# One core: bulk loads of a spectral filter and a gated MLP moved from ScalarE's queue to SyncE's, the late ones held back to points of the matmul order

## The chip, the cores and the metric

The kernel runs on one core of a Trainium2 chip. Five engines work beside each other, each on its own instruction stream: TensorE (PE) multiplies matrices, VectorE (DVE) and ScalarE (ACT) do elementwise work, GpSimd (POOL) does small things, and SyncE (SP) issues DMAs. ScalarE can issue DMAs too; such an instruction stands in its stream like any other. The metric is the device time of one execution in microseconds.

## The reference

`x` is 2048 by 512. The result is the sum of the input, a global spectral filter of the normalised input (2D FFT, multiplication by a complex weight, inverse FFT) and a gated MLP of the normalised input:

```python
def _A_ref(x, w_r, w_i):
    X = jnp.fft.rfft2(x.astype(jnp.float32), axes=(-2, -1))
    X = X * (w_r + 1j * w_i)                              # 2048 x 257
    return jnp.fft.irfft2(X, s=(S, D), axes=(-2, -1)).astype(jnp.bfloat16)

def _B_ref(x, w_gate, w_up, w_down):                      # 512 -> 1792 -> 512
    h = _gelu(x @ w_gate) * (x @ w_up)
    return h @ w_down

xn = _layernorm(x)
return x + _A_ref(xn, A_w_r, A_w_i) + _B_ref(xn, B_w_gate, B_w_up, B_w_down)
```

## The kernel before

The rows of `x` form 16 tiles of 128, taken as four blocks of four. Each tile is normalised (`xn`), transposed by TensorE into PSUM and copied to `xnT`. For block 0 two of the four copies are VectorE's (L364) and two ScalarE's (L366); for blocks 1 to 3 all are VectorE's.

The MLP is the spine of the program: for each block b and each of 14 columns of weights fc there is a `gate` (four matmuls, a GELU on ScalarE) and an `up` (four matmuls, a product on VectorE), and from block 1 on four `down`s work off the block before. Between these stand *hooks*, numbered in order of the program: 28 in block 0, 40 in each later block. The table `plan` says which pieces of the filter are issued at which hook (`at(h, ...)`):

- `unit_D(j)` and `unit_A(j)`, hooks 4 to 43: the two forward transforms of tile j. `unit_D` needs the constants `fd`; `unit_A` needs `am` (which lies in `arena`), and ends with ScalarE's copy into one of four buffers `tt`, a store of it to the DRAM tensor `scr1`, and a load of the store before it into `tv`. Both DMAs are SP's.
- `unit_B(h)`, hooks 46 to 91: the last forward step and the multiplication by the weights. Needs all of `tv`, `be`, and `Wr`, `Wi` on VectorE.
- `unit_C(h)`, hooks 50 to 95, needs `cm`; it goes through `scr2` into `vv`. `unit_E`, `unit_F` from hook 101 on; `unit_F` needs `gm`. `down` needs `wd`, from hook 34 on.

Each engine runs its list in the order in which the Python code calls `op(engine, ...)`. `op` works out the semaphore waits from the keys an instruction reads (`r`) and writes (`w`), and puts them in front of it. A DMA is one such instruction: the engine that issues it goes on once the queue has taken it.

At the start, TensorE runs 24 matmuls on a zeroed tile `dumm` (`warm`, L327) while the first rows come in. The loads are written at the head of the function. Those of the first half of `x` and the first weight pieces are shared between SP and ScalarE; of the later ones SP has the rest of `x`, `fd` and one weight piece, ScalarE all others, 18 in all.

Of the kernel before, what the change touches and what calls it, by code (L numbers as in the profile page):

```python
# [7 lines left out]
ACT = mybir.ActivationFunctionType  # L8
# [7 lines left out]
KD = 257  # L16
FF = 1792
P = 128
NJ = 16
# [90 lines left out]
class _Prog:  # L110
# [14 lines left out]
            self.cnt[e] = 0  # L125
        self.dsem = []

    def op(self, eng, fn, r=(), w=(), dma=False):
        deps = []
        for k in r:  # L130
            if k in self.writer:
                deps.append((self.writer[k], True))
        for k in w:
            if k in self.writer:
                deps.append((self.writer[k], False))
            for ev in self.readers.get(k, ()):
                deps.append((ev, False))
        need = {}
        for (st, val), raw in deps:
            if st == eng and not dma and (eng == "pe" or not raw):  # L140
                continue
            need[st] = max(need.get(st, 0), val)
        known = self.known[eng]
        need = {s: v for s, v in need.items() if known.get(s, 0) < v}
        need = {s: v for s, v in need.items()
                if not any(s2 != s and self.clk[(s2, v2)].get(s, 0) >= v for s2, v2 in need.items())}
        for s, v in need.items():
            for a, b in self.clk[(s, v)].items():
                if known.get(a, 0) < b:
                    known[a] = b  # L150
        if dma:
            st = next((d for d in self.dsem if known.get(d, 0) >= self.cnt[d]), None)
            if st is None:
                st = "d%d" % len(self.dsem)
                self.sem[st] = self.es.enter_context(self.nc.semaphore("s_" + st))
                self.cnt[st] = 0
                self.dsem.append(st)
            self.cnt[st] += 16
            ev, inc = (st, self.cnt[st]), 16
            clk = dict(known)  # L160
        else:
            self.cnt[eng] += 1
            ev, inc = (eng, self.cnt[eng]), 1
            clk = dict(self.lastclk[eng])
            for a, b in known.items():
                if clk.get(a, 0) < b:
                    clk[a] = b
        clk[ev[0]] = ev[1]
        self.clk[ev] = clk
        if not dma:  # L170
            self.lastclk[eng] = clk
        self.q[eng].append((fn, list(need.items()), ev[0], inc))
        for k in r:
            self.readers.setdefault(k, []).append(ev)
        for k in w:
            self.writer[k] = ev
            self.readers[k] = []
        return ev
# [12 lines left out]
def bass_parallel_sum__spectral_gfnet__glu_gated_geglu__prompt_kernel(  # L191
# [12 lines left out]
    c_fd = nc.inline_tensor(FD_np, name="c_fd")  # L204
    c_am = nc.inline_tensor(AM_np, name="c_am")
    c_be = nc.inline_tensor(BE_np, name="c_be")
    c_cm = nc.inline_tensor(CM_np, name="c_cm")
    c_g = nc.inline_tensor(G_np, name="c_g")
# [5 lines left out]
    wgv = B_w_gate.rearrange("(dc p) f -> p dc f", p=P)  # L214
    wuv = B_w_up.rearrange("(dc p) f -> p dc f", p=P)
    wdv = B_w_down.rearrange("(fc p) d -> p fc d", p=P)

    with ExitStack() as es:
# [3 lines left out]
        pr = _Prog(nc, es)  # L222
        op = pr.op
# [6 lines left out]
        am = arena[:, 0:4096].rearrange("p (j r c) -> p j r c", j=NJ, r=2)  # L230
# [4 lines left out]
        wg_sb = sb("wg", [P, 4, FF], BF16)  # L235
        wu_sb = sb("wu", [P, 4, FF], BF16)
        wd_sb = sb("wd", [P, NFC, D], BF16)
        hT = [sb("hT%d" % i, [P, NFC, 512], BF16) for i in range(2)]
        ident = sb("ident", [P, P], F16)
        fd = sb("fd", [P, 768], F16)  # L240
        be = sb("be", [P, 2 * P], F16)
        cm = sb("cm", [P, 16, 2, P], F16)
        gm = sb("gm", [P, 4, 256], F16)
# [38 lines left out]
        def dma(eng, dst, src, r=(), w=()):  # L282
            return op(eng, lambda e: e.dma_start(dst, src), r=r, w=w, dma=True)  # L283

        def load_x(j0, n, b, eng):
            dma(eng, x_sb[64 * b:64 * b + 64, j0:j0 + n, :], xv[b, :, j0:j0 + n, :], w=[("x", j, b) for j in range(j0, j0 + n)])

        def load_w(t, v, nm, lo, hi, eng):
            dma(eng, t[:, :, P * lo:P * hi], v[:, :, P * lo:P * hi], w=[(nm, i) for i in range(lo, hi)])
# [8 lines left out]
        load_w(wu_sb, wuv, "wu", 0, 2, "sp")  # L298
        for b, eng in ((0, "sp"), (1, "act")):
            load_x(4, 4, b, eng)  # L300
        load_w(wg_sb, wgv, "wg", 2, 6, "sp")
        load_w(wu_sb, wuv, "wu", 2, 6, "act")
        dma("sp", fd[:], c_fd.ap(), w=["fd"])
        dma("act", am, c_am.ap().rearrange("p (j r c) -> p j r c", j=NJ, r=2), w=["am"])
        load_x(8, 4, 0, "sp")
        load_x(8, 4, 1, "sp")
        load_w(wg_sb, wgv, "wg", 6, 10, "act")
        load_w(wu_sb, wuv, "wu", 6, 10, "act")
        load_x(12, 4, 0, "sp")
        load_x(12, 4, 1, "sp")  # L310
        load_w(wg_sb, wgv, "wg", 10, 14, "act")
        load_w(wu_sb, wuv, "wu", 10, 14, "act")
        dma("act", wd_sb[:], wdv, w=["wd"])
        dma("act", be[:], c_be.ap(), w=["be"])
        for t, src, nm in ((Wr, A_w_r, "Wr"), (Wi, A_w_i, "Wi")):
            v = src.rearrange("(m hh h) k -> hh m h k", hh=2, h=16)
            for hh in range(2):
                dma("act", t[64 * hh:64 * hh + 64, :, 0:KD], v[hh], w=[(nm, hh)])
        dma("act", cm[:], c_cm.ap().rearrange("p (j r c) -> p j r c", j=16, r=2), w=["cm"])
        dma("act", gm[:], c_g.ap().rearrange("p (a c) -> p a c", a=4), w=["gm"])  # L320


        def warm(n):
# [136 lines left out]
        def unit_C(h):  # L460
            bk = 5
            y = yy[h % 4]

            def fn(e):
                ins = None
                for ri in range(2):
                    for hh in range(2):
                        ins = e.matmul(bank(bk + hh)[:, 0:257], cm[64 * hh:64 * hh + 64, h, ri, :], y[64 * hh:64 * hh + 64, ri, 0:KD],  # L468
                                       start=(ri == 0), stop=(ri == 1), skip_group_check=True)
                return ins  # L470

            op("pe", fn, r=["cm", ("yy", h % 4, 0), ("yy", h % 4, 1)], w=[("ps", bk), ("ps", bk + 1)])
            v4 = vp[h % 4]
            op("act", lambda e: e.activation(v4[:], pair(bk), ACT.Copy), r=[("ps", bk), ("ps", bk + 1)], w=[("vp", h % 4)])  # L474
            dma("sp", scr2.rearrange("(h b y) (x c) -> h (y x) b c", b=2, y=4, c=KD)[h], v4[:], r=[("vp", h % 4)], w=[("scr2", h)])
            if h > 0:
                load_vv(h - 1)
            if h == 15:
                load_vv(h)
# [100 lines left out]
        def down(b, jj):  # L580
            j = 4 * b + jj
            bk = 7

            def part(f0, f1):
                def fn(e):
                    ins = None
                    for fc in range(f0, f1):
                        ins = e.matmul(bank(bk), hT[b % 2][:, fc, jj * P:(jj + 1) * P], wd_sb[:, fc, :], start=(fc == 0), stop=(fc == NFC - 1))  # L588
                    return ins
                op("pe", fn, r=["wd"] + [("hT", b % 2, fc) for fc in range(f0, f1)], w=[("ps", bk)])  # L590

            part(0, 5)
            hook()
            part(5, 10)
            hook()
            part(10, 14)

            def add(dst, key):
                op("dve", lambda e: e.tensor_tensor(dst, bank(bk), x_sb[:, j, :], ALU.add), r=[("ps", bk), ("acc", j), ("x", j, 0), ("x", j, 1)], w=[key])  # L599
            if j in fin_done:  # L600
                store(j, lambda t, key: add(t[:], key))
            else:
                add(x_sb[:, j, :], ("acc", j))
                acc_done[j] = True
            hook()
# [5 lines left out]
        def at(h, *calls):  # L611
            plan.setdefault(int(h), []).extend(calls)
# [5 lines left out]
        def hook(fl=True):  # L618
# [3 lines left out]
            if fl:  # L622
                flush()

        for m in range(1, 4):
            a = 10 * (m - 1)
            for i in range(4):
                at(a + i, (ln_stat, 4 * m + i))
            at(a + 3, (ln_aggr, 4 * m, 4))
            for i in range(4):  # L630
                at(a + 6 + i // 2, (ln_norm, 4 * m + i))
            at(a + 8, (trans, m, (0, 1), (0, 1, 2, 3), 7))
            at(a + 9, (trans, m, (2, 3), (0, 1, 2, 3), 7))
            at(a + 10, (butter, m, 0))
            at(a + 11, (butter, m, 1))
# [88 lines left out]
```

## Time and profile before

| | |
|---|---|
| median of three executions | 251.59 us (249.69 to 252.6) |
| the profiled execution | 252.13 us, its span 250.3 us |
| granted TensorE clock, mean over the span | 0.916 |
| TensorE matmul busy | 198.6 us, 79% |
| VectorE busy | 113.3 us, 45% |
| ScalarE busy | 90.6 us, 36% |
| HBM read / written | 16.57 MB / 6.31 MB |
| SP's queue (q1) / ScalarE's queue (q10) | 13.12 MB / 9.77 MB |

The profile comes from one execution. Busy shares do not count the issuing of DMAs: an engine that is held up while it issues a load shows as idle, and its issue stands in the timeline as SPq or ACTq. The rows with two numbers in front give start and duration in microseconds; a bracket at the end gives the idle time ahead of the instruction and what ended it. The list of waits gives the total, how often, and the longest. The rows of windows give the busy time of each engine, the granted clock of TensorE, the busy share of the DMA engines and what they moved in GB/s. A chain of waits is followed back from the last instruction.

### The profile page before, as it was taken

The numbers are of one execution on the slowest core, as the hardware profiler recorded it, in microseconds if no ns is written. First come the engines' busy times: TensorE is split into PE (matmuls) and PEld (weight loads), VectorE is DVE, ScalarE is ACT, GpSimd is POOL, SyncE is SP. The second block draws the span as 40 slices with busy tenths as digits, with TensorE's granted clock in tenths as the row PEclk, the third lists the DMA queues.
The fourth block names the chain that finished last, engine by engine and source line by source line (L and its number), as shares of the span: only waits on it lengthen the run. The fifth ranks groups of instructions, "written<-read, shape, count | busy, mean of one in ns | idle before, by whom it ended". The sixth has DMA issues, their size and how long they took to land.

```text
span 250.3 us, 3084 instructions
## 1 busy us (share of the span) xinstructions
PE 198.6 (79%) x1131; PEld 89.9 (36%) x1145; DVE 113.3 (45%) x262; ACT 90.6 (36%) x157; POOL 9.3 (4%) x26
## 2 busy tenths in 40 slices
PE   8600000799999999849999999998799999999973
PEld 2300000245444444313333333343355555555421
DVE  3600000487878733206666666463046455365421
ACT  0000001654546446304445535433155446454100
POOL 0200000010101000000000000000000000000000
PEclk9965555699999999979999999999799999999999
DMA  6999999901333333300233313323001111100001
GB/s 175 294 315 291 347 155 151 240 31 43 94 78 85 84 87 84 84 21 21 53 76 84 83 47 84 81 68 84 1 12 46 31 42 43 43 21 25 21 21 42
DMA packets 23695, 23.09 MB, mean 92 GB/s; under 512 B 1920, under 2 KB 22400, under 8 KB 23168
## 3 DMA queue, kind: packets, MB, share of 16 engines
q1 hardware_dynamic: 13728, 13.12, 21.1%
q10 hardware_dynamic: 9952, 9.77, 17.0%
q8 instruction: 9, 0.15, 0.3%
q14 instruction: 6, 0.05, 0.1%
HBM read 16.57 MB, written 6.31 MB: 91 GB/s over the span
## 4 chain that ended last, share of the span: by engine, by line
PE 71%; ACTq 17%; DMA 5%; DVE 3%; ACT 1%; issue 1%
PE ps L575 19%; PE ps L588 19%; PE ps L562 18%; ACTq L283 17%; PE ps L442 2%; PE ps L468 2%; PE ps L501 2%; DMA tv<-scr 1%; PE ps L418 1%; PE ps L354 1%; DMA arena<-scr 1%; DMA scr<-tt 1%; DVE osb L599 1%; DMA scr<-vp 1%; DVE hT L578 1%
## 5 line engine op out<-in xcount | busy, mean ns | idle before, releaser
L562 PE MATMUL ps<-xnT,wg 128*128 128x512 f16 x224 | 58.8, 386 | 35.1 <-ACT xnT L366 35.1
L578 DVE TENSOR_TENSOR hT<-ps,gl 128x512 bf16<-128x512 f32 x56 | 38.6, 690 | 45.9 <-PE ps L575 41.7
L575 PE MATMUL ps<-xnT,wu 128*128 128x512 f16 x224 | 59.0, 387 | 0.0
L588 PE MATMUL ps<-wd,hT 128*128 128x512 bf16 x210 | 52.2, 388 | 3.1 <-DVE osb L599 1.9
L565 ACT ACTIVATE gl<-ps 128x512 bf16<-128x512 f32 x56 | 33.4, 597 | 42.9 <-PE ps L562 42.2
L562 PEld LDWEIGHTS ps<-xnT,wg 128*128 128x128 bf16 x224 | 20.7, 99 | 58.5 <-issue 39.9
L588 PEld LDWEIGHTS ps<-wd,hT 128*128 128x128 bf16 x224 | 20.8, 99 | 26.9 <-issue 4.1
L575 PEld LDWEIGHTS ps<-xnT,wu 128*128 128x128 bf16 x224 | 20.7, 99 | 23.0 <-issue 5.0
L376 DVE TENSOR_TENSOR arena<-xnT 128x1024 f16<-128x1024 f16 x4 | 2.8, 693 | 33.5 <-ACT xnT L366 33.4
L366 ACT ACT_TABLE_LOAD x1 | 1.3, 1283 | 42.9 <-issue 42.9
L599 DVE TENSOR_TENSOR x_sb<-ps,x_sb 128x512 bf16<-128x512 f32 x11 | 7.6, 691 | 19.9 <-PE ps L588 19.9
L448 ACT ACTIVATE xc<-ps 128x514 f16<-128x514 f32 x16 | 9.6, 600 | 15.0 <-PE ps L442 15.0
L508 ACT ACTIVATE zt<-ps 128x512 bf16<-128x512 f32 x16 | 9.5, 595 | 10.4 <-PE ps L501 10.4
L428 ACT ACTIVATE tt<-ps 128x514 f16<-128x514 f32 x16 | 9.6, 598 | 10.1 <-PE ps L422 10.1
L535 ACT ACTIVATE eo<-ps 128x512 bf16<-128x512 f32 x16 | 9.5, 595 | 9.2 <-PE ps L530 9.2
L333 DVE BATCH_NORM_STATS2 st<-x_sb 128x6 f32<-128x512 bf16 x16 | 10.6, 684 | 3.8 <-DMA x_sb<-in_A_x_dram 3.8
L474 ACT ACTIVATE vp<-ps 128x514 bf16<-128x514 f32 x16 | 9.6, 598 | 7.3 <-PE ps L468 7.3
L401 ACT ACTIVATE xs<-ps 128x512 f16<-128x512 f32 x16 | 9.5, 596 | 4.3 <-PE ps L397 4.3
L442 PE MATMUL ps<-tv,be 128*64 128x257 f16 x64 | 6.8, 294 | 4.4 <-DMA tv<-scr 4.4
L509 POOL COPY zt<-xn 1x128 bf16<-1x128 bf16 x16 | 4.5, 283 | 146.9 <-ACT zt L508 146.9
L327 PE MATMUL ps<-dumm 128*128 128x512 f16 x24 | 8.2, 524 | 1.2 <-DVE dumm L291 1.2
L540 DVE TENSOR_TENSOR ys<-eo 128x256 bf16<-128x256 bf16 x16 | 4.6, 289 | 9.3 <-ACT eo L535 9.3
(59 smaller groups left out, 156.9 us busy)
## 6 DMA issues: line engine op xcount, KB each, us to landing
scr<-tt SPq DMA_DIRECT2D x16, 128.5 KB
tv<-scr SPq DMA_DIRECT2D x16, 128.5 KB
scr<-vp SPq DMA_DIRECT2D x16, 128.5 KB
arena<-scr SPq DMA_DIRECT2D x16, 128.5 KB
out_dram<-osb SPq DMA_DIRECT2D x32, 64.0 KB
wd<-in_B_w_down_dram ACTq DMA_DIRECT2D x1, 1792.0 KB, 16.7
wu<-in_B_w_up_dram ACTq DMA_DIRECT2D x3, 512.0 KB, 17.3
x_sb<-in_A_x_dram SPq DMA_DIRECT2D x5, 256.0 KB, 15.0
```

The source lines that it names most:

```text
L283: return op(eng, lambda e: e.dma_start(dst, src), r=r, w=w, dma=True)
L333: op("dve", lambda e: e.bn_stats(st[:, j, :], x_sb[:, j, :]), r=[("x", j, 0), ("x", j, 1)], w=[("st", j)])
L428: op("act", lambda e: e.activation(t4[:], pair(bk), ACT.Copy, scale=SC_A), r=[("ps", bk), ("ps", bk + 1)], w=[("tt", j % 4)])
L442: ins = e.matmul(bank(bk + ri)[64 * hh:64 * hh + 64, 0:257], be[:, 64 * ri:64 * ri + 64], tv[:, 16 * hh + h, :], start=True, stop=True, sk ...
L448: op("act", lambda e: e.activation(xc[s2][:, :, 0:KD], pair(bk), ACT.Copy, scale=SC_B), r=[("ps", bk), ("ps", bk + 1)], w=[("xc", s2)])
L474: op("act", lambda e: e.activation(v4[:], pair(bk), ACT.Copy), r=[("ps", bk), ("ps", bk + 1)], w=[("vp", h % 4)])
L562: ins = e.matmul(bank(bg), wg_sb[:, dc, fc * P:(fc + 1) * P], xnT[:, dc, b * 512:(b + 1) * 512], start=(dc == 0), stop=(dc == 3))
L565: op("act", lambda e: e.activation(gl[k % 2][:], bank(bg), ACT.Gelu_apprx_tanh), r=[("ps", bg)], w=[("gl", k % 2)])
L575: ins = e.matmul(bank(bu), wu_sb[:, dc, fc * P:(fc + 1) * P], xnT[:, dc, b * 512:(b + 1) * 512], start=(dc == 0), stop=(dc == 3))
L578: op("dve", lambda e: e.tensor_tensor(hT[b % 2][:, fc, :], bank(bu), gl[k % 2][:], ALU.mult), r=[("ps", bu), ("gl", k % 2)], w=[("hT", b % ...
L588: ins = e.matmul(bank(bk), hT[b % 2][:, fc, jj * P:(jj + 1) * P], wd_sb[:, fc, :], start=(fc == 0), stop=(fc == NFC - 1))
L599: op("dve", lambda e: e.tensor_tensor(dst, bank(bk), x_sb[:, j, :], ALU.add), r=[("ps", bk), ("acc", j), ("x", j, 0), ("x", j, 1)], w=[key])
```

## The change

The loads of the head, but for the first four of ScalarE, are written for SP, in the order in which they are needed. ScalarE gets a GELU on one column of `dumm` in their place. The loads of `wd` (in four pieces), `be`, `Wr`, `Wi`, `cm` (in two pieces) and `gm` are taken out of the head and entered in the plan, at hooks 10 to 52: `load_late` issues them from SP with a wait until TensorE has finished everything that stands ahead of this hook. `wd` and `cm` get keys by piece, so that their readers wait for the piece they need.

```diff
-    def op(self, eng, fn, r=(), w=(), dma=False):
-        deps = []
+    def op(self, eng, fn, r=(), w=(), dma=False, after=()):
+        deps = [(ev, True) for ev in after]
...
+        def load_late(dst, src, keys):
+
+            op("sp", lambda e: e.dma_start(dst, src), w=keys, dma=True, after=[("pe", pr.cnt["pe"])])
...
             load_x(4, 4, b, eng)
+        op("act", lambda e: e.activation(dumm[:, 0:1], mhalf[:, 0:1], ACT.Gelu_apprx_tanh), r=["mhalf"], w=["dumm"])
+        dma("sp", fd[:], c_fd.ap(), w=["fd"])
         load_w(wg_sb, wgv, "wg", 2, 6, "sp")
-        load_w(wu_sb, wuv, "wu", 2, 6, "act")
-        dma("sp", fd[:], c_fd.ap(), w=["fd"])
-        dma("act", am, c_am.ap().rearrange("p (j r c) -> p j r c", j=NJ, r=2), w=["am"])
+        load_w(wu_sb, wuv, "wu", 2, 6, "sp")
         load_x(8, 4, 0, "sp")
         load_x(8, 4, 1, "sp")
-        load_w(wg_sb, wgv, "wg", 6, 10, "act")
-        load_w(wu_sb, wuv, "wu", 6, 10, "act")
+        dma("sp", am, c_am.ap().rearrange("p (j r c) -> p j r c", j=NJ, r=2), w=["am"])
+        load_w(wg_sb, wgv, "wg", 6, 10, "sp")
+        load_w(wu_sb, wuv, "wu", 6, 10, "sp")
         load_x(12, 4, 0, "sp")
         load_x(12, 4, 1, "sp")
-        load_w(wg_sb, wgv, "wg", 10, 14, "act")
-        load_w(wu_sb, wuv, "wu", 10, 14, "act")
-        dma("act", wd_sb[:], wdv, w=["wd"])
-        dma("act", be[:], c_be.ap(), w=["be"])
-        for t, src, nm in ((Wr, A_w_r, "Wr"), (Wi, A_w_i, "Wi")):
-            v = src.rearrange("(m hh h) k -> hh m h k", hh=2, h=16)
-            for hh in range(2):
-                dma("act", t[64 * hh:64 * hh + 64, :, 0:KD], v[hh], w=[(nm, hh)])
-        dma("act", cm[:], c_cm.ap().rearrange("p (j r c) -> p j r c", j=16, r=2), w=["cm"])
-        dma("act", gm[:], c_g.ap().rearrange("p (a c) -> p a c", a=4), w=["gm"])
+        load_w(wg_sb, wgv, "wg", 10, 14, "sp")
+        load_w(wu_sb, wuv, "wu", 10, 14, "sp")
...
-            op("pe", fn, r=["cm", ("yy", h % 4, 0), ("yy", h % 4, 1)], w=[("ps", bk), ("ps", bk + 1)])
+            op("pe", fn, r=[("cm", h), ("yy", h % 4, 0), ("yy", h % 4, 1)], w=[("ps", bk), ("ps", bk + 1)])
...
-                op("pe", fn, r=["wd"] + [("hT", b % 2, fc) for fc in range(f0, f1)], w=[("ps", bk)])
+                op("pe", fn, r=[("wd", fc) for fc in range(f0, f1)] + [("hT", b % 2, fc) for fc in range(f0, f1)], w=[("ps", bk)])
...
+        for i in range(4):
+            f0, f1 = (0, 4, 8, 11, 14)[i:i + 2]
+            at(10 + 2 * i, (load_late, wd_sb[:, f0:f1, :], wdv[:, f0:f1, :], [("wd", fc) for fc in range(f0, f1)]))
+        at(18, (load_late, be[:], c_be.ap(), ["be"]))
+        for i, (t, src, nm) in enumerate(((Wr, A_w_r, "Wr"), (Wi, A_w_i, "Wi"))):
+            v = src.rearrange("(m hh h) k -> hh m h k", hh=2, h=16)
+            for hh in range(2):
+                at(19 + 3 * (2 * hh + i), (load_late, t[64 * hh:64 * hh + 64, :, 0:KD], v[hh], [(nm, hh)]))
+        cmv = c_cm.ap().rearrange("p (j r c) -> p j r c", j=16, r=2)
+        for i in range(2):
+            at(31 + 3 * i, (load_late, cm[:, 8 * i:8 * i + 8], cmv[:, 8 * i:8 * i + 8], [("cm", h) for h in range(8 * i, 8 * i + 8)]))
+        at(52, (load_late, gm[:], c_g.ap().rearrange("p (a c) -> p a c", a=4), ["gm"]))
```

What moves shows best in the engines' lists. The rows give the line, the operation, what it writes and reads, its shape, and the semaphores it waits for. First ScalarE before, from the eleventh of its 18 loads up to the first GELU. `wd` is the down weight, `be`, `cm`, `gm` constants, `Wr` and `Wi` the filter's weights, `xnT` the transposed input and `gl` the GELU's output:

```order
L283 DMA wd<-in_B_w_down_dram 128x14x512
L283 DMA be<-c_be 128x256
L283 DMA Wr<-in_A_w_r_dram 64x16x257 x2
L283 DMA Wi<-in_A_w_i_dram 64x16x257 x2
L283 DMA cm<-c_cm 128x4096
L283 DMA gm<-c_g 128x1024
L366 ACT_TABLE_LOAD
L366 ACTIVATE xnT<-ps 128x2x256 [waits s_pe] x2
L565 ACT_TABLE_LOAD
L565 ACTIVATE gl<-ps 128x512 [waits s_pe] x2
```

And ScalarE after, from its start:

```order
L283 DMA x_sb<-in_A_x_dram 64x1024 x2
L283 DMA wg<-in_B_w_gate_dram 128x4x256
L283 DMA x_sb<-in_A_x_dram 64x2048
L305 ACT_TABLE_LOAD [waits s_dve]
L305 ACTIVATE dumm<-mhalf 128x1 [waits s_pool]
L363 ACTIVATE xnT<-ps 128x2x256 [waits s_pe] x2
L562 ACTIVATE gl<-ps 128x512 [waits s_pe] x2
```

Fourteen loads are gone from ahead of the copies, and one table load stands ahead of both instead of one ahead of each. On TensorE the start reads like this before, where `dumm` is the zeroed tile of the warm-up:

```order
L327 MATMUL ps<-dumm 128x512 [waits s_dve]
L327 MATMUL ps<-dumm 128x512 x23
L354 MATMUL ps<-ident,xn 128x128 [waits s_dve,s_d4]
L354 MATMUL ps<-ident,xn 128x128 x7
L354 MATMUL ps<-ident,xn 128x128 [waits s_dve]
```

And after:

```order
L324 MATMUL ps<-dumm 128x512 [waits s_act]
L324 MATMUL ps<-dumm 128x512 x23
L351 MATMUL ps<-ident,xn 128x128 [waits s_dve,s_d4]
L351 MATMUL ps<-ident,xn 128x128 x7
L351 MATMUL ps<-ident,xn 128x128 [waits s_dve]
```

The order is the same; the first matmul waits for ScalarE in place of VectorE. SP, in the stretch of the first unit_A tiles (`scr` is the DRAM scratch, `tt` and `tv` what is stored to it and loaded from it), before:

```order
L283 DMA fd<-c_fd 128x768
L283 DMA x_sb<-in_A_x_dram 64x2048 x4
L283 DMA scr<-tt 128x2x257 [waits s_act] x2
L283 DMA tv<-scr 8x8224 [waits s_d0]
L283 DMA scr<-tt 128x2x257 [waits s_act]
L283 DMA tv<-scr 8x8224 [waits s_d1]
L283 DMA scr<-tt 128x2x257 [waits s_act]
L283 DMA tv<-scr 8x8224 [waits s_d2]
```

And after, from the last loads of the head on:

```order
L283 DMA wg<-in_B_w_gate_dram 128x4x512
L283 DMA wu<-in_B_w_up_dram 128x4x512
L283 DMA scr<-tt 128x2x257 [waits s_act] x2
L283 DMA tv<-scr 8x8224 [waits s_d0]
L287 DMA wd<-in_B_w_down_dram 128x4x512 [waits s_pe]
L283 DMA scr<-tt 128x2x257 [waits s_act]
L283 DMA tv<-scr 8x8224 [waits s_d1]
L287 DMA wd<-in_B_w_down_dram 128x4x512 [waits s_pe]
L283 DMA scr<-tt 128x2x257 [waits s_act]
```

The held-back loads stand between the scr stores and tv loads, each behind a wait for TensorE (`s_pe`).

## The prediction

> **What bounds the kernel now.** I read the busy tenths of the page first, to see where TensorE stands still:
>
> ```profile
> PE   8600000799999999849999999998799999999973
> PEclk9965555699999999979999999999799999999999
> ```
>
> One slice is 6.26 us. TensorE works in slices 1 and 2, is idle from about 12 to 44 us, and from there on is nine tenths busy to the end, with two short dips. The list of waits names the hole:
>
> ```profile
> PE ps L562 <- ACT xnT L366: 35.1, 1, 35.1
> ACT L366 <- issue: 42.9, 1, 42.9
> PE ps L442 <- DMA tv<-scr: 4.4, 1, 4.4
> ```
>
> The first gate matmul (L562) waits 35.1 us for ScalarE's copy of the transposed input (L366); ScalarE itself "waits" 42.9 us for nothing but its own issue. The timeline of ScalarE says what it issues:
>
> ```profile
> 2.02 0.85 ACTq L283 DMA_DIRECT2D wg<-in_B_w_gate_dram  x1
> 2.90 0.54 ACTq L283 DMA_DIRECT2D x_sb<-in_A_x_dram  x1
> ...
> 7.16 5.39 ACTq L283 DMA_DIRECT2D wg<-in_B_w_gate_dram  x1
> 12.58 5.88 ACTq L283 DMA_DIRECT2D wu<-in_B_w_up_dram  x1
> ...
> 42.38 0.45 ACTq L283 DMA_DIRECT2D gm<-c_g  x1
> 42.86 1.28 ACT L366 ACT_TABLE_LOAD   x1 [42.86 <-issue]
> 44.15 1.08 ACT L366 ACTIVATE xnT<-ps 128x512 f16<-128x512 f16 x2
> 45.26 1.28 ACT L565 ACT_TABLE_LOAD   x1
> ```
>
> Up to 7 us a load takes ScalarE 0.5 to 1.2 us to issue; from 7.16 on each takes up to 6 us, as the queue takes new loads only as fast as old ones land. So the two copies, whose input was in PSUM at 10.3, begin at 44.15. TensorE's own rows, and VectorE's last normalisation, give what was ready when:
>
> ```profile
> 1.19 8.24 PE L327 MATMUL ps<-dumm 128*128 128x512 f16 x24 [1.19 <-DVE dumm L291]
> 8.53 0.73 DVE L345 TENSOR_SCALAR xn<-x_sb,ag,rstd 128x512 f16<-128x512 bf16 x2 [0.27 <-POOL rstd L341]
> 9.26 1.06 PE L354 MATMUL ps<-ident,xn 128*128 128x128 f16 x16
> 45.38 1.86 PE L562 MATMUL ps<-xnT,wg 128*128 128x512 f16 x4 [35.06 <-ACT xnT L366]
> ```
>
> From 45.38 to the end, 204.9 us, the kernel is bound by TensorE, and the change adds no arithmetic there. So the question is when the first gate starts, and whether the loads that it needs then keep up.
>
> **Term 1, the start of the first gate.** ScalarE keeps its first four loads, unchanged in place, so it has issued them at 2.90 + 0.54 = 3.44. Now the table load and a 128x1 GELU follow. The table load is 1.28. The shortest ACTIVATE of the trace is this:
>
> ```profile
> L489 ACT ACTIVATE row<-ps 32x64 bf16<-32x64 f32 x1 | 0.2, 212 | 2.9 <-PE ps L487 2.9
> ```
>
> I take 0.21 and end at 4.98. The GELU writes `dumm`, which the 24 warm-up matmuls read. They waited for VectorE's memset before and wait for ScalarE now: TensorE starts at about 5.1 instead of 1.19 (0.15 for the hand-over, as between the copies' end, 45.23, and the gate). This is the one cost that the change puts on the path. With 8.24 for the warm-up, TensorE gets to the transposes at 13.35, though `xn` is ready at 9.26 as before. The 16 transposes take 1.06, to 14.4. The second copy needs the last of them: half of 1.08, so 15.0, and 0.15 on top. The first gate starts at about 15.2 instead of 45.38: **30.2 us less**. Both old table loads are covered by the one new; the second cost nothing before, since its GELU waited for the gate matmuls anyway.
>
> Its bounds hang on the clock in the warm-up. The weight loads show it: they come 0.43 us apart until 7.11, then nine of them within 1.82:
>
> ```profile
> 6.71 0.15 PEld L327 LDWEIGHTS ps<-dumm 128*128 128x128 f16 x1 [0.28 <-issue]
> 7.11 1.82 PEld L327 LDWEIGHTS ps<-dumm 128*128 128x128 f16 x9 [0.25 <-issue]
> ```
>
> So TensorE was slow for 5.9 us there. The second slow stretch is shorter (columns: window, length, busy time of each engine, granted clock, DMA share, GB/s):
>
> ```profile
> 45.38:48.40 3.02, 3.02 (x9) 1.09 (x10) 1.25 (x2) 1.76 (x2) 0.00 (x0) 0.56 1.04 290
> 48.40:50.20 1.80, 1.80 (x9) 0.71 (x8) 1.60 (x4) 0.60 (x1) 0.00 (x0) 1.00 0.56 222
> ```
>
> At 0.56 of the clock, about 2.8 us were slow. With 2.8 us slow, the warm-up is 2.8/0.43 = 6.5 slow matmuls and 17.5 at 1.80/8 = 0.225, 6.7 in all: 1.5 us sooner. With 5.9 it is the 8.24. I take 8.24, the row of the same instructions, and keep 1.5 us less for the range. The Trainium skill, "TensorE: Matmul & The Clock Gate", Part 1: The HAM clock gate, says that a free-running window of about 3.4 us of activity must pass at half clock. By that the warm-up could be slow for anything from 3.4 to 6.8 us, and 8.24 could become 6.9 to 8.6. The first stretch, 5.9, agrees; the second, 2.8, is shorter than a whole window.
>
> **Term 2, the first gates at full clock.** Before, the first eight matmuls took 3.02 us where the next eight took 1.80, since TensorE had been idle for 35 us. In the changed kernel only about 0.8 us lie between the transposes and the gate, and before the clock was still up well after the transposes ended at 10.3:
>
> ```profile
> 12.00:14.00 2.00, 0.00 (x0) 0.00 (x0) 0.00 (x0) 0.00 (x0) 0.00 (x0) 0.97 1.04 409
> 14.00:16.00 2.00, 0.00 (x0) 0.00 (x0) 0.00 (x0) 0.00 (x0) 0.00 (x0) 0.50 1.06 350
> ```
>
> So these eight run at 1.80: **1.2 us less**.
>
> **Term 3, the early loads on one queue.** SP now issues all of `x`, `fd`, `am` and both weights. What TensorE needs first and could miss is `am` (1024 KB), for the first unit_A:
>
> ```profile
> arena<-c_am ACTq DMA_DIRECT2D x1, 1024.0 KB
> 53.21 0.28 PE L418 MATMUL ps<-xs,arena 64*128 64x257 f16 x2
> ```
>
> It came 7.8 us after the first gate, 6.6 without the slow clock: 21.8 in the changed kernel. Up to and with `am` both queues carry x 0..11 (1536 KB), `ident` 32, `fd` 192, the first and second weight pieces 1536 and `am` 1024: 4320 KB, 4.42 MB. The rates that the trace shows for such loads:
>
> ```profile
> 6.00:8.00 2.00, 2.00 (x9) 0.73 (x8) 1.97 (x8) 0.00 (x0) 0.99 (x2) 1.00 0.98 228
> 24.00:30.00 6.00, 0.00 (x0) 0.00 (x0) 0.00 (x0) 0.00 (x0) 0.00 (x0) 0.50 1.10 348
> 31.00:46.00 15.00, 0.62 (x2) 0.28 (x3) 0.66 (x2) 3.11 (x4) 0.00 (x0) 0.50 1.25 159
> ```
>
> From 2 us on, at 228 GB/s `am` lands at 21.4, at 348 at 14.7; the weights 10..13 (7.05 MB in all) at 32.9 or 22.3, long before their turn at hook 20. **Nothing**, between nothing and 8 us (159 GB/s puts `am` at 29.8); I take the near rows, as the 159 stretch is `Wr`, `Wi` in rows of 514 bytes. SP itself is free once its last early load is taken. If it runs three 512 KB loads ahead of the landings, as ScalarE did at 7.16 (an estimate: `wu`, `wg`, `wu` were just issued and could not have landed), that is when 5.48 MB have landed, between 17.7 and 26.0 by the two rates. The first `scr` store is due 9.05 - 1.2 = 7.9 us after the gate, at 23; up to 3 us late it holds nobody, as four `tt` buffers stand ahead of it.
>
> ```profile
> 54.43 3.89 SPq L283 DMA_DIRECT2D scr<-tt  x2
> ```
>
> **Term 4, the loads held back.** `wd`, `be`, `Wr`, `Wi`, `cm`, `gm` go to SP behind waits for TensorE's count at hooks 10 to 52. A hook takes (102.15 - 53.21)/37 = 1.32 us (last and first unit_A, hooks 43 and 6). All are long ahead of their readers: `wd` at hook 34, `Wr` at 46, `cm` at 50, `gm` at 105. The waits themselves hold nothing up: each point lies in TensorE's order ahead of the unit_A whose store stands behind it on SP. The cost can only lie in the bytes ahead of the scr stores and tv loads in the queue:
>
> ```profile
> 102.15 0.28 PE L418 MATMUL ps<-xs,arena 64*128 64x257 f16 x2
> 54.00:103.00 49.00, 47.09 (x317) 22.41 (x317) 31.46 (x66) 26.19 (x47) 2.01 (x2) 1.00 0.33 79
> 103.21 3.02 DMA scr<-tt
> 106.25 3.49 DMA tv<-scr
> ```
>
> The thick part is hooks 19 to 31, 15.9 us, with four loads of 514 KB: 13.2 us at 159 GB/s, beside 0.33 x 15.9 = 5.2 us of scr and tv traffic. The queue falls 2.5 us behind. A store then takes 3.0 (the chain's row) + 3.3 (one load ahead of it) + 2.5 = 8.8 us, and the store of unit_A(j) has to land before ScalarE writes the same of four `tt` buffers, 10 hooks or 13.2 us later. So nothing stops; and from hook 31 on only 1 MB of `cm` comes, so the lag is gone by hook 43. What may remain is a later last tv load, on which unit_B already waits 4.4 us. Bounds 0 and 3.3 (one load ahead of it); I take **0.5 us more**, near zero, as `cm` is issued 9 hooks earlier.
>
> **Sum.** 250.3 - 30.2 - 1.2 + 0 + 0.5 = 219.4 of span. The profiled execution took 252.13, so 1.8 lie around its span: 221.2, say 221. That execution is 0.5 above the median of the runs shown, 251.59, by which it would be 220.7.
>
> **The rivals.**
> A shorter warm-up: TensorE reaches full clock after 2.8 us, not 5.9. Then 221.2 - 1.5 = 219.7. For it the second slow stretch, against it the first, which are the same instructions.
>
> SP falls behind between hooks 19 and 31: at 140 GB/s (my estimate of the lower end of the 159 stretch) the four loads take 15.0, the lag is 4.3 and a load ahead 3.8, and SP also waits for each scr store before the tv load that follows; should the two lags come on top of each other, ScalarE stops at `tt`, and with it the GELUs behind it and TensorE. Up to 8 us: 225 to 229. For it the thin slack, against it the four buffers.
>
> `am` late: 159 GB/s for one queue puts it 8 us late, 229. Against it the 348 GB/s between 24 and 30, when only ScalarE's queue still had loads, since SP's last four were issued by 8.69 and its x loads landed within 15.4:
>
> ```profile
> 5.86 2.83 SPq L283 DMA_DIRECT2D x_sb<-in_A_x_dram  x4
> DMA to landing us min/median/max: 14.7/15.0/15.4
> ```
>
> The other sign: one queue does not carry the loads. If SP's queue moved 79 GB/s, as in the row from 54 to 103, `am` would land at 58, 36 us late, and the time would be 257. It decides below 4.42 MB/(21.8 + 30.9 - 2) = 87 GB/s. Against it, the same 348; the 79 is what was asked for there, at a DMA share of 0.33.
>
> A rule against the change: the Trainium skill, "DMA: Bandwidth & Descriptors", Issuing engines are not separate DMA queues, says that the issuer matters little, only the sequencer's issue time, usually small beside the transfer, is saved. By the short issue rows (about 0.6 for each of 14 loads moved) that would save 8 us and give 244. The trace differs: those loads held ScalarE from 3.47 to 42.83. I give it no more than the rest below.
>
> **Chances.** Forecast 0.57, shorter warm-up 0.13, SP behind 0.2, `am` late 0.06, the other sign 0.01, the rest 0.03. The range 218.3 to 226.5 holds the first two, with 1.4 us below for the copies and the hand-over, and most of the third. About 1% is what a measurement of this kernel can tell from no change. All cases but the other sign and part of the rest are faster by far more: faster 0.98, same 0.01, slower 0.01.
>
> **What would show it.** The first gate at about 15.2, behind a warm-up that starts at about 5.1 and waits for ScalarE; ScalarE's issue over by 3.5, with one table load; the first gates at clock 1.0; no wait of L418's counterpart for `arena`; unit_B's wait for tv near 4.4; no long wait of ScalarE for the `tt` stores. The prediction is wrong if the first gate starts after 18, or if the stretch from the first gate to the end is longer than before's 204.9.

## The result and the profile after

The changed kernel takes 228.69 us, median of four (227.11 to 232.68), beside 250.64 for the kernel before: a ratio of 0.910, 95% interval 0.900 to 0.920. It is faster by some 22 us, where 30 were forecast; the range ended at 226.5. The profiled execution took 228.33, its span 226.5. Some executions, here and below (one of these four, at 232.68), were in a slower state; the medians hold them, the ratios leave them out.

The busy tenths of the page, one slice now 5.66 us:

```profile
PE   1989898999976805999999999997999999999883
DMA  6999869799995640042231322330011102101011
```

The long hole at the start is gone. A new one stands in slices 13 to 16, from 68 to 90 us, and ahead of it the DMA engines are busy nearly without a break; before, they had been done with the loads at 50 us and were a third busy after that. The start, from the timeline (start, duration, engine, line, operation):

```profile
3.23 1.28 ACT L305 ACT_TABLE_LOAD   x1 [3.23 <-issue]
4.52 0.20 ACT L305 ACTIVATE dumm<-mhalf 128x1 f16<-128x1 f32 x1
4.78 7.76 PE L324 MATMUL ps<-dumm 128*128 128x512 f16 x24 [4.78 <-ACT dumm L305]
12.38 1.06 PE L351 MATMUL ps<-ident,xn 128*128 128x128 f16 x16
13.03 1.08 ACT L363 ACTIVATE xnT<-ps 128x512 f16<-128x512 f16 x2 [8.30 <-PE ps L351]
14.26 1.02 PE L559 MATMUL ps<-xnT,wg 128*128 128x512 f16 x4 [0.82 <-ACT xnT L363]
```

The first gate starts at 14.26 and the matmuls run at full clock from the first (1.02 us for four, against 1.86). So much was foreseen. What came after it shows in the waits (total, times, longest), first of the engines, then of SP's queue:

```profile
PE ps L439 <- DMA tv<-scr: 8.7, 1, 8.7
ACT tt L425 <- DMA scr<-tt: 7.6, 3, 4.9
PE ps L559 <- ACT gl L562: 3.7, 1, 3.7
```

```profile
SPq L283 <- DMA scr<-tt: 33.1, 12, 4.6
SPq L287 <- PE ps L559: 2.0, 4, 0.6
```

ScalarE waits for the stores of `tt`; a gate waits for a GELU that stands behind this wait on ScalarE; unit_B waits 8.7 us for `tv` instead of 4.4; and SP stands 33 us on stores, but hardly on the waits for TensorE that the change put in. Cut at unit_B's first matmul, the two profiles compare like this (window, length, busy time by engine, granted clock, DMA share, GB/s), the changed kernel first, the kernel before second:

```profile
14.26:87.36 73.10, 58.97 (x369) 27.11 (x369) 38.27 (x83) 29.84 (x53) 3.02 (x3) 0.94 0.85 179
87.36:226.50 139.14, 131.22 (x737) 58.45 (x737) 68.56 (x162) 57.03 (x100) 4.53 (x16) 0.98 0.19 48
```

```profile
45.38:109.87 64.49, 58.17 (x366) 27.05 (x369) 38.26 (x82) 31.09 (x54) 3.02 (x3) 0.98 0.34 87
109.87:250.30 140.43, 131.33 (x725) 58.86 (x737) 68.52 (x162) 57.03 (x100) 4.53 (x16) 0.97 0.19 46
```

The start gave 45.38 - 14.26 = 31.1 us. The stretch from the first gate to unit_B gave back 73.10 - 64.49 = 8.6, or 9.9 if the 1.3 us of the first gates at half clock are taken off before. Behind unit_B 1.3 us were gained. 250.3 - 31.1 + 8.6 - 1.3 = 226.5. So the question of the experiments is the 9.9.

Most of it is waiting, but not all. The gate's wait of 3.7 is new, and unit_B's is 4.2 longer (8.65 instead of 4.41). Behind the first of these waits TensorE's clock fell; the windows from 70 to 76 of the changed kernel, with the granted clock third from the end:

```profile
70.00:72.00 2.00, 1.91 (x12) 0.79 (x13) 0.69 (x1) 1.18 (x4) 0.00 (x0) 0.78 0.62 182
72.00:74.00 2.00, 2.00 (x7) 0.83 (x6) 0.00 (x0) 1.03 (x2) 0.00 (x0) 0.50 0.30 71
74.00:76.00 2.00, 2.00 (x12) 0.67 (x11) 0.69 (x1) 0.17 (x1) 0.00 (x0) 0.86 0.87 253
```

That is (0.22 + 0.50 + 0.14) x 2 = 1.7 us of full clock lost. 3.7 + 4.2 + 1.7 = 9.6 of the 9.9.

How SP works through that stretch shows in its own timeline:

```profile
45.65 1.03 SPq L283 DMA_DIRECT2D scr<-tt  x1
50.36 0.57 SPq L283 DMA_DIRECT2D tv<-scr  x1
50.97 0.66 SPq L287 DMA_DIRECT2D Wr<-in_A_w_r_dram  x1
51.68 1.31 SPq L283 DMA_DIRECT2D scr<-tt  x1
56.50 0.57 SPq L283 DMA_DIRECT2D tv<-scr  x1
57.11 0.65 SPq L287 DMA_DIRECT2D Wi<-in_A_w_i_dram  x1
57.81 1.05 SPq L283 DMA_DIRECT2D scr<-tt  x1
62.43 0.57 SPq L283 DMA_DIRECT2D tv<-scr  x1
63.04 0.44 SPq L287 DMA_DIRECT2D cm<-c_cm  x1
63.53 0.76 SPq L283 DMA_DIRECT2D scr<-tt  x1
68.88 0.55 SPq L283 DMA_DIRECT2D tv<-scr  x1
```

The stores are those of tiles 7, 8, 9 and 10, the tv loads those of 6 to 9. A tv load can be issued when the store of its own tile has landed: the store of tile 8, issued at 51.68, lands by 62.43, 10.7 us later, that of tile 9 takes 11.1. While SP stands there, it issues neither the next late load nor the next store, though `tt` is ready. Each turn takes 6.1 us, and TensorE makes a tile in 3.3. ScalarE's side of it:

```profile
48.04 0.59 ACT L425 ACTIVATE tt<-ps 128x514 f16<-128x514 f32 x1
51.56 0.60 ACT L425 ACTIVATE tt<-ps 128x514 f16<-128x514 f32 x1 [0.92 <-PE ps L419]
...
62.49 0.60 ACT L425 ACTIVATE tt<-ps 128x514 f16<-128x514 f32 x1 [2.54 <-DMA scr<-tt]
...
68.95 0.60 ACT L425 ACTIVATE tt<-ps 128x514 f16<-128x514 f32 x1 [4.88 <-DMA scr<-tt]
```

Tile 9's `tt` was ready at 52.16, its store was issued at 57.81 and landed at 68.88: 16.7 us from ready to landed. Tile 13 uses the same buffer, four tiles or some 13 us later, and its copy waits 4.88. Two theories, then. *Bandwidth*: the DMA engines are full while `Wr` and `Wi` come in rows of 514 bytes, and nothing on SP's order can help. *Coupling*: a store is slow since it stands behind a late load on the one queue, and SP multiplies this by waiting for it.

### The profile page after: what moved, and what is told of

The parts are those of the page before. It is cut to its first block, busy times and chain, and to the rows that moved or that the text cites. A ratio compares the mean times of both kernels' runs of the same rounds, so it can differ in the third digit from the quotient of the medians.

```text
span 226.5 us, 3103 instructions
## 1 busy us (share of the span) xinstructions
PE 198.8 (88%) x1145; PEld 89.4 (39%) x1145; DVE 113.2 (50%) x262; ACT 89.4 (39%) x157; POOL 9.3 (4%) x26
## 4 chain that ended last, share of the span: by engine, by line
PE 74%; DMA 16%; DVE 3%; ACT 2%; ACTq 1%; issue 1%; SPq 1%
PE ps L585 19%; PE ps L572 19%; PE ps L559 18%; DMA scr<-tt 12%; PE ps L324 3%; PE ps L439 3%; PE ps L465 2%; PE ps L498 2%; DMA tv<-scr 2%; PE ps L351 1%; DMA arena<-scr 1%; DVE osb L596 1%; DMA scr<-vp 1%; ACTq L283 1%; PE ps L415 1%; DVE hT L575 1%
## 5 line engine op out<-in xcount | busy, mean ns | idle before, releaser
L585 PE MATMUL ps<-wd,hT 128*128 128x512 bf16 x224 | 53.7, 381 | 1.9 <-DVE osb L596 1.9
L596 DVE TENSOR_TENSOR osb<-ps,x_sb 128x512 bf16<-128x512 f32 x5 | 3.5, 691 | 10.3 <-PE ps L585 10.3
L439 PEld LDWEIGHTS ps<-tv,be 128*64 128x64 f16 x64 | 2.3, 110 | 15.5 <-issue 12.9
```

The source lines that it names most:

```text
L439: ins = e.matmul(bank(bk + ri)[64 * hh:64 * hh + 64, 0:257], be[:, 64 * ri:64 * ri + 64], tv[:, 16 * hh + h, :], start=True, stop=True, sk ...
```

## The experiments

Each run has the kernel before beside it on the same chip, and the ratio goes by that. The table gives the median, the ratio to before with its interval, and from the profiles the first gate, unit_B's first matmul, and the time between.

| | median us | ratio to before | first gate | unit_B | between |
|---|---|---|---|---|---|
| before | | 1 | 45.38 | 109.87 | 64.5 |
| the change | 228.69 | 0.910 [0.900, 0.920] | 14.26 | 87.36 | 73.1 |
| warm-up freed | 229.96 | 0.914 [0.907, 0.921] | 10.82 | 87.04 | 76.2 |
| tv load of tile j-3 | 223.95 | 0.888 [0.880, 0.896] | 14.65 | 82.46 | 67.8 |
| W rows in one run | 223.97 | 0.890 [0.883, 0.897] | 13.71 | 81.37 | 67.7 |
| W loads split | 229.60 | 0.911 [0.905, 0.916] | 13.47 | 88.03 | 74.6 |
| late loads on GpSimd | 230.16 | 0.913 [0.902, 0.924] | 13.53 | 88.16 | 74.6 |
| stores on ScalarE | 224.34 | 0.896 [0.891, 0.902] | 13.85 | 81.19 | 67.3 |
| nothing held back | 238.78 | 0.948 [0.936, 0.961] | 14.16 | 97.89 | 83.7 |
| no wait for TensorE | 230.02 | 0.911 [0.906, 0.915] | 13.31 | 86.80 | 73.5 |
| tv of j-3 and W rows | 220.55 | 0.881 [0.878, 0.883] | 14.48 | 78.80 | 64.3 |
| the same, warm-up freed | 219.93 | 0.879 [0.873, 0.886] | 11.05 | 78.65 | 67.6 |
| the same, `am` cut, tv caught up | 215.01 | 0.860 [0.855, 0.864] | 10.95 | 73.90 | 63.0 |

### The tv load of an older tile

```diff
-            if j > 0:
-                load_tv(j - 1)
+            if j >= 3:
+                load_tv(j - 3)
             if j == NJ - 1:
-                load_tv(j)
+                for i in range(j - 2, NJ):
+                    load_tv(i)
```

> The tv load of tile j-3 instead of j-1 stands behind the store of tile j, so SP does not wait for a store that it has just issued. Theory of coupling (each store stands in the queue behind a late load, and SP, waiting for it, issues nothing else, so a tile takes 6 us of SP's time instead of 3.3): ScalarE no longer waits for tt stores, unit_B waits 4 to 6 us instead of 8.7, span 217 to 220. Theory of bandwidth (the DMA engines are full with rows of 514 bytes between 44 and 68 us): the stores land as late as now, span 224.5 to 226.5.

Measured: span 223.1. SP's wait for stores fell from 33.1 to 10.4, ScalarE's for `tt` from 7.6 to 2.8, unit_B's from 8.7 to 7.4; between gate and unit_B 5.3 us went. Coupling is at work, but not all of it: the span lies between what the two theories said.

### W rows in one run

```diff
-        Wr = sb("Wr", [P, 16, 258], BF16)
-        Wi = sb("Wi", [P, 16, 258], BF16)
+        Wr = sb("Wr", [P, 16, 257], BF16)
+        Wi = sb("Wi", [P, 16, 257], BF16)
```

> Wr and Wi get tiles of 257 columns instead of 258, so that 16 rows of a partition are one run of 8224 bytes. Theory of bandwidth: a W load of 514 KB takes about 1.7 us (300 GB/s) instead of 3.5, the stall of hooks 19 to 43 goes, span 217 to 219. Theory of coupling: the store behind it lands sooner too, but SP still takes one round trip per tile, 3 + 1.7 us instead of 6 against 3.3 us of TensorE: half of the loss stays, span 221 to 223. In both, the products on VectorE (L454's counterpart) may take longer on odd rows.

Measured: span 221.3, inside what the coupling theory gave (221 to 223). ScalarE waits for no `tt` at all, but SP still waits 30.4 us for stores, and unit_B 8.9 for `tv`. The window from 44 to 60 of the changed kernel and of this one, in this order:

```profile
44.00:60.00 16.00, 15.43 (x106) 7.49 (x106) 10.51 (x24) 8.53 (x15) 1.01 (x1) 1.00 1.12 142
```

```profile
44.00:60.00 16.00, 15.43 (x104) 7.54 (x103) 9.95 (x23) 8.51 (x15) 1.01 (x1) 1.00 0.92 194
```

The same engines, busy for less of the time, move 194 GB/s instead of 142 once a partition's W is one run of 8224 bytes. And SP's turns get shorter, though it still waits for each store:

```profile
45.00 0.56 SPq L283 DMA_DIRECT2D tv<-scr  x1
...
46.17 0.58 SPq L283 DMA_DIRECT2D scr<-tt  x1
49.79 0.56 SPq L283 DMA_DIRECT2D tv<-scr  x1
...
50.97 0.58 SPq L283 DMA_DIRECT2D scr<-tt  x1
54.20 0.56 SPq L283 DMA_DIRECT2D tv<-scr  x1
...
58.11 0.56 SPq L283 DMA_DIRECT2D tv<-scr  x1
```

4.4 us in place of 6.1. The tv loads at 54.20 and 58.11 are those of the stores at 46.17 and 50.97, so a store lands in 8.0 and 7.1 us instead of 10.7 to 11.1. VectorE's products, feared slower on odd rows, take 428 ns as before (427 and 430).

### W in smaller pieces

```diff
-                at(19 + 3 * (2 * hh + i), (load_late, t[64 * hh:64 * hh + 64, :, 0:KD], v[hh], [(nm, hh)]))
+                for q in range(2):
+                    at(19 + 3 * (2 * hh + i) + 1.5 * q, (load_late, t[64 * hh:64 * hh + 64, 8 * q:8 * q + 8, 0:KD], v[hh][:, 8 * q:8 * q + 8], [(nm, hh, q)]))
```

> Each of the four W loads is cut into two of 8 rows, 1.5 hooks apart; bytes and row lengths are the same. Theory of coupling: a store has half a load ahead of it, 1.8 us less per round trip for the tiles between hooks 19 and 31, span 221 to 224. Theory of bandwidth: no change, span 226 to 227.

(The products on VectorE then wait for their half alone; these lines are not shown.)

Measured: span 227.8, and `tt` waits of 9.3 us. But the run does not test what was expected of it. `at` takes whole hooks (`int(h)`), so the halves stand at hooks 19 and 20, 22 and 23, and so on, and in SP's timeline both halves of the first three loads are issued together, with no store between them:

```profile
45.58 1.38 SPq L287 DMA_DIRECT2D Wr<-in_A_w_r_dram  x2
47.00 0.62 SPq L283 DMA_DIRECT2D scr<-tt  x1
```

As much stands ahead of these stores as before. Only the last load is parted by a store (issued at 60.44, landed by 67.61), and one store decides nothing. What half a load ahead of a store would do stays open.

### Another queue, for the loads or for the stores

In one kernel the late loads go to GpSimd's queue (the lines for its semaphores are not shown), in the other the store of unit_A goes to ScalarE's:

```diff
-            op("sp", lambda e: e.dma_start(dst, src), w=keys, dma=True, after=[("pe", pr.cnt["pe"])])
+            op("pool", lambda e: e.dma_start(dst, src), w=keys, dma=True, after=[("pe", pr.cnt["pe"])])
```

> The held-back loads are issued by GpSimd, on a queue of its own, at the same points; SP keeps only the scr stores and tv loads. Theory that the order on one queue is what costs (a store stands behind a late load): the stores no longer stand behind W, ScalarE's wait for tt stores goes from 7.6 us to under 1, and unit_B starts 5 to 8 us sooner than 87.4; span 218 to 221. Theory of bandwidth: the same bytes share the same engines, unit_B starts at 84 to 87, span 223 to 227.

```diff
-            dma("sp", scr1.rearrange("(j b y) (x c) -> j (y x) b c", b=2, y=4, c=KD)[j], t4[:], ...)
+            dma("act", scr1.rearrange("(j b y) (x c) -> j (y x) b c", b=2, y=4, c=KD)[j], t4[:], ...)
```

> Only the scr store of unit_A moves, to ScalarE's queue, which holds nothing after 3 us; the tv loads stay on SP behind the late loads. Theory of the order on one queue: a store lands about 3 to 4 us after its issue, ScalarE never waits for tt, SP's wait for stores falls from 33 us to under 10; unit_B still waits for the last tv loads; span 217 to 221, with some 0.4 us of issue per tile on ScalarE hidden. Theory of bandwidth: a store still takes 8 us between 44 and 68, span 223 to 226.

With the late loads away from SP, its stores get slower still, and the span of 228.0 is beyond both forecasts (the waits of the GpSimd kernel, of SP's queue first and then of ScalarE):

```profile
SPq L284 <- DMA scr<-tt: 41.8, 13, 14.1
```

```profile
ACT tt L426 <- DMA scr<-tt: 11.3, 2, 9.1
```

This run changes more than the place, though: GpSimd's queue stands in the profile as another kind (`software_dynamic`, where SP's is `hardware_dynamic`). The other run does not have this flaw. With the stores on a queue that holds nothing but stores they are as slow as on SP's: that of tile 8 is issued at 48.26, and its tv load at 59.44. Both rows are of this kernel's timeline:

```profile
48.26 0.37 ACTq L283 DMA_DIRECT2D scr<-tt  x1
...
59.44 0.55 SPq L283 DMA_DIRECT2D tv<-scr  x1
```

11.2 us, on a queue that held only the store before it; SP's wait for stores, forecast to fall under 10, rose to 41.9. So the late loads ahead of it on its queue are not what makes a store slow, and that half of the coupling theory is refuted. What fits in its place is that the engines which all queues share are full (a DMA share of 1.15 from 44 to 60 in this kernel). The Trainium skill, "DMA: Bandwidth & Descriptors", Issuing engines are not separate DMA queues, says that transfers interleave on the same 16 engines whoever issues them; both runs agree. Yet the kernel with the stores on ScalarE has no `tt` wait and unit_B starts 6 us sooner: the stores are slow, but they are issued when `tt` is ready, not 3 to 6 us later.

### What the holding back is worth

All late loads at the head, on SP, in the same order:

```diff
+        dma("sp", wd_sb[:], wdv, w=[("wd", fc) for fc in range(NFC)])
+        dma("sp", be[:], c_be.ap(), w=["be"])
...
+        dma("sp", gm[:], c_g.ap().rearrange("p (a c) -> p a c", a=4), w=["gm"])
```

> Nothing is held back: wd, be, Wr, Wi, cm, gm are loads of the head, on SP, behind the weights. Theory of bandwidth: the DMA engines finish the loads by about 48 to 50 us as in the kernel before, the first scr store lands only then, ScalarE stops at the fifth tt (about 34) until 50, and from there the stores meet an empty queue, unit_A(15) 36 us later: unit_B starts at 90 to 94, span 229 to 233. If the hold-back is worth nothing, span 226 to 227; if it costs, below 225.

Measured: 238.78, span 236.9. The mechanism is as expected, larger by a few us (229 to 233 was forecast): SP is held by its own loads until 46.67, and ScalarE then stops at `tt` in one piece (SP's timeline, then the list of waits):

```profile
46.67 1.37 SPq L283 DMA_DIRECT2D scr<-tt  x2
```

```profile
ACT tt L433 <- DMA scr<-tt: 20.0, 1, 20.0
```

So the move off ScalarE's queue, with the new start, is worth about 12 us of the 22 (250.64 - 238.78), and the holding back, added to it, about 10 (238.78 - 228.69). And the wait for TensorE's count, taken away with the loads left in their places (`after=` dropped):

> The held-back loads keep their places on SP, between the stores and the tv loads, but lose the wait for TensorE. SP's waits for TensorE in the changed kernel sum to under 5 us, against 33 for stores: if the place in SP's order holds the loads back, and the wait does not, nothing changes, span 225.5 to 227.5. If the wait itself costs, below 224.

Measured: span 227.0, median 230.02. The wait is worth nothing that shows; what is left to hold the loads back is their place between the stores.

### An earlier start

```diff
-        op("act", lambda e: e.activation(dumm[:, 0:1], mhalf[:, 0:1], ACT.Gelu_apprx_tanh), r=["mhalf"], w=["dumm"])
+        op("act", lambda e: e.activation(pre[:, 0:1], mhalf[:, 0:1], ACT.Gelu_apprx_tanh), r=["mhalf"], w=["pre"])
```

> The GELU that preloads the table writes a tile of its own, so the warm-up no longer waits for ScalarE. Theory (the start shift is worth its size): the warm-up starts at 1.2 again, the first gate at about 11.3 instead of 14.26, span 226.5 - 3.0 = 223.5. Rival (the stall between hooks 19 and 43 is set by when the DMA engines get through the bytes, not by when TensorE starts): the gate starts 3 us earlier, but the wait of ScalarE for the tt stores and of unit_B for tv grow by as much, span 225.5 to 226.5.

Measured: the gate starts 3.4 us earlier, at 10.82, and the span is 227.6. TensorE gives 3.1 us of it back ahead of unit_B, in a wait of 2.0 for `am` and in longer `tt` waits (10.5 instead of 7.6), and the end is no earlier. The start of unit_B was not set by TensorE's start but by the loads and SP's turns. Then the two edits that helped, together, without and with the free warm-up:

> The tv load of tile j-3 and W rows of one run, with the warm-up still behind the GELU. With both, no store is late: ScalarE waits for no tt. If an earlier first gate is worth its size once the queue keeps up, this is 2 to 3 us slower than e8_best: span 221.5 to 222.5, unit_B at 81. If the bytes of the early loads set the pace, equal to e8_best: span 219 to 220.

> The warm-up freed, the tv load of tile j-3, and W rows of one run, all three together. If the free warm-up was worth nothing only because the DMA queue set the start of unit_B, it is worth its 3 us once the queue keeps up: first gate at 10.8, unit_B at 75 to 78, span 214 to 217. If the early loads are the bound, unit_B stays near 80 and the span at 218 to 221.

With both edits SP waits 0.8 us for stores, nobody waits for `tt`, and 64.3 us lie between gate and unit_B. The kernel before has 64.5 with, and 63.2 without, the half clock of its first gates. So 8.8 of the 9.9 are found; the 1.1 that stays is unit_B's wait for `tv`, 5.5 instead of 4.4. The free warm-up on top is worth nothing that shows again, but by another cause, since ScalarE waits for no `tt` in either. The timeline of TensorE in that kernel:

```profile
19.88 0.28 PE L416 MATMUL ps<-xs,arena 64*128 64x257 f16 x2 [2.22 <-DMA arena<-c_am]
...
20.55 1.91 PE L574 MATMUL ps<-xnT,wu 128*128 128x512 f16 x4
22.25 1.87 PE L561 MATMUL ps<-xnT,wg 128*128 128x512 f16 x4
```

It waits 2.2 us for `am`, and the eight matmuls behind the wait run at half clock, 1.9 us for four where 1.03 is usual: 2.2 + 1.7 = 3.9, against the 3.4 of the earlier start. This is one execution, the slowest of four (221.19) and at the lowest mean clock (0.967, the others 0.981 to 0.984); that the clock fell there in the others too is not shown. So the last kernel takes the first 6 tiles of `am` ahead of x 8..11 and the rest behind the weights 6..9, and issues the last tv loads in pairs:

```diff
+        dma("sp", am[:, 0:6], amv[:, 0:6], w=[("am", 0)])
         load_x(8, 4, 0, "sp")
...
+        dma("sp", am[:, 6:16], amv[:, 6:16], w=[("am", 1)])
...
+            for i in {13: (10, 11), 14: (12, 13), 15: (14, 15)}.get(j, (j - 3,)):
+                if i >= 0:
+                    load_tv(i)
```

> e8_best, and am in two loads, the first (tiles 0 to 5) ahead of x 8..11, and the last tv loads caught up so that only two are issued after the last store. If the 2.2 us wait for am and the 1.2 us of unit_B's wait above the 4.4 of the kernel before are real terms: no wait for am, unit_B at 75.5 to 77 with a wait near 4.5, span 215.5 to 217. If the DMA engines are the bound up to unit_B, the waits move and the span stays at 219.

Measured: span 213.2, median 215.01 us, the fastest of all, and below the 215.5 to 217 that were forecast. No wait for `am` is left, unit_B starts at 73.90 after a wait of 4.2, and between gate and unit_B lie 63.0 us, close to the 63.2 of before without the slow first gates. How much each of the two edits gives is not taken apart. Of its lead over the kernel ahead, 1.5 us lie behind unit_B (139.3 instead of 140.8), where the clock did not fall this time (see *Behind unit_B* below).

## Why the prediction was partly right, and where it failed

*The start of the first gate: right, a little small.* 31.1 us instead of 30.2. ScalarE's loads were issued by 3.14, the GELU ended at 4.72, the warm-up ran 4.78 to 12.54. It took 7.76 us, between the two bounds, 6.7 and 8.24; over all runs it took 6.8 to 8.2. The Trainium skill, "TensorE: Matmul & The Clock Gate", Part 1: The HAM clock gate, gives a window of about 3.4 us, from which the prediction had 6.9 to 8.6 as an estimate; the runs agree but for 0.1 us at the lower end.

*The first gates at full clock: right.* 1.3 us for 1.2.

*The early loads: right, with no room.* `am` was not waited for. In the run with split W, whose gate started 0.8 us earlier, TensorE waited for it until 21.3, which is what the row of 228 GB/s had given (21.4).

*The loads held back: here it failed.* The step is "A store then takes 3.0 (the chain's row) + 3.3 (one load ahead of it) + 2.5 = 8.8 us ... So nothing stops", with 0.5 us as its term. It was 9.9, with 1.7 of fallen clock in it that the term did not have at all. Two things in it were wrong. A store took 10.7 to 11.1 us instead of 8.8, and not because a late load stood ahead of it in its queue, as the sum's 3.3 has it: on ScalarE's queue it took 11.2. It got shorter, 7.1 to 8.0, when the rows of W got longer. How full engines make one store wait so long is not shown. And the sum counted from the issue, while SP issued the store 3.0 and 5.7 us after `tt` was ready, being held by the store before. Ready to landed is 13.8 and 16.7 us, past the 13.2 of the four buffers. The prediction named this wait, "SP also waits for each scr store before the tv load that follows", but only in the rival. This rival, at 225 to 229 and with a chance of 0.2, is what happened. The wait of 8.7 us at unit_B is the rest of the same lag, which the term had as gone by hook 43. Three of the prediction's own signs say so: ScalarE did wait for the `tt` stores, unit_B waited 8.7 instead of near 4.4, and the stretch from the first gate to the end took 226.5 - 14.26 = 212.2 us, longer than the 204.9 of before. The miss would have been larger, had not the start (0.9), the first gates (0.1) and the stretch behind unit_B (1.3) come out shorter than forecast.

Both factors count: take away SP's wait, or its late issue of the stores, or the short rows, and 5 to 6 us of the 9.9 go; take away SP's wait and the short rows, and 8.8 go.

*The other rivals.* From 2 to 20 us the DMA engines moved 245 to 334 GB/s, nearly all of it for SP's queue (ScalarE's moved 0.79 MB in the whole run), so the rival of the other sign had no ground. That issue rows of 0.6 us would bound the gain did not hold for the start; that all issuers share the same engines did, as the two runs with another queue show.

*Slips in the working.* 3.44 + 1.28 + 0.21 is 4.93, not 4.98. A clock of 0.56 over 3.02 us makes 2.7 us at half clock, not 2.8. One issue of ScalarE, that of `be`, took 6.74 us, more than "up to 6". And `am` was among the loads just issued at 7.16, so more than three loads of 512 KB were ahead of the landings; SP was free at 16.95, ahead of the 17.7 to 26.0. None of them bears on the step that failed.

*Behind unit_B.* That this stretch is 1.3 us shorter is a matter of the clock, not of the change. TensorE waits there for `vv`, 2.45 us before and 2.22 after. Before, the clock fell behind this wait (granted 0.50 from 178 to 180 us and 0.71 to 182); after, it stayed at 1.00. Nine matmuls of `down` took 3.39 us there before (at 178.56) and 2.10 after (at 156.03).

In the seven profiles in which the clock fell at this place, the kernel before among them, the stretch takes 140.2 to 140.8 us; in the six others 139.0 to 139.9. The length of the wait does not decide it: it fell behind waits of 2.2 to 2.8 us and stayed behind waits of 2.2 to 2.7. Spans of single profiles can differ by as much for this reason alone; the column "between" is free of it.

## What to carry to other kernels

Where an engine issues loads for others, look how long its issue takes once the queue is full; it may be held for as long as the loads last. When bulk loads move behind a store-and-reload chain, count the chain's time from data ready to buffer free, with the issuer's own waits in it, and let the issuer wait only for stores that are several turns old. Before buying an earlier start, look which bytes the start will then wait for.

## What the runs showed of the hardware

A pause of 2.2 us was once enough for TensorE's clock to fall: in the kernel with the freed warm-up and both edits the granted clock was 0.64 from 20 to 22 us and 0.51 from 22 to 24, behind the wait for `am`. Behind the 2.0 us wait at the same place in the kernel with the freed warm-up alone it stayed at 1.00. But a length that decides can't be read from this: it also stayed at 1.00 behind the wait of 2.2 us for `vv` in the changed kernel, and fell behind the same wait of 2.45 in the kernel before.

With W in rows of 514 bytes the engines moved about a fourth less: 142 GB/s in the window from 44 to 60 with them, 194 with runs of 8224 bytes, the traffic of the stores in both.
